# First tile's v loads moved to other queues, and w_in's first quarter issued between v's chunks

## The chip, the cores and the metric

The kernel runs on one core of one Trainium2 chip. The metric is the time of one execution on the device in microseconds (us). It is about 1.7 us longer than the span from the first to the last instruction, which is what the profile shows. Each ratio compares a kernel with runs of the kernel before on the same chip; the two chips are called A and B.

In the lines from profiles, PE is TensorE (the matmuls and transposes), ACT is ScalarE, DVE is VectorE, POOL is GpSimd and SP is SyncE; a q after the name (ACTq, SPq) is that engine's sequencer, here busy with issuing a transfer. PSUM is where this kernel keeps the tiles that PE writes (`hp`, `ops` and `sc` in the lines). The semaphore of a transfer is the number under which the trace records its landing; each load of the head has 16 updates there, and counts here as landed at the last. The granted clock is the profile's column of that name: 1.0 or 0.5 in these records. Fillers are matmuls whose result nobody uses.

## The reference, cut to what matters

```python
# q, k, v: 8 batches x 8 heads x 576 positions x 64, float32
scores = (1/sqrt(64)) * q @ k^T
ret    = scores * where(i >= j, gamma[h] ** (i - j), 0)     # retention: a decay per head
attn   = ret @ v
x      = attn as (4608 tokens, 512)
h      = x @ w_in                    # 512 x 2048
g      = h * tanh(softplus(h))       # Mish
out    = g @ w_out                   # 2048 x 512
```

## The kernel before

The tokens go in tiles of four chunks of 128 positions. The first tile's four chunks are the head of the kernel: nothing can be multiplied before their q and k are loaded, so that tile is loaded and prepared by its own code. q and k of a chunk are four transfers on SyncE's queue, and v is one on ScalarE's:

```python
def load_first(n):
    b, i0, _ = chunks[n][0]
    m, u = divmod(n, 2)
    for x, src in (("q", q), ("k", k)):
        heads = src.rearrange("b (p e) s d -> b e p s d", e=2)
        for e in range(2):
            nc.sync.dma_start(out=pairs[m][x][:, u, ds(4 * e, 4), :]..., in_=heads[b, e, :, ds(i0, P), :]...)
    nc.scalar.dma_start(out=pairs[m]["v"][:, u], in_=v[b, :, ds(i0, P), :].rearrange("h p d -> p h d"))

load_first(0)
# ...
keep_warm(12)                                     # filler matmuls on PE, so that it never stands idle for long
# ... small constants; two exponentials on ScalarE ...
nc.scalar.activation(gv, ex, AX.Exp, scale=-1.0)
nc.scalar.activation(gq, ex, AX.Exp)
nc.vector.tensor_scalar(gq, gq, 1.0 / math.sqrt(D), None, op0=OP.mult)
load_first(1)                                     # <- v1's issue stands here in ScalarE's queue
first = consts.tile([P, 1], F32)
nc.scalar.activation(first, pos[:, 0:1], AX.Mish) # fetches the Mish table early
```

A chunk then passes through these steps: P (VectorE scales q into bfloat16), C (GpSimd casts k), V (GpSimd scales v), T (transposes), S (scores and the mask), O (outputs). PE transposes q into a PSUM tile, ScalarE copies it out, and only then does PE write k's half of the same tile (in the profile of before the copy ends at 11.01 and k's transposes start at 11.05):

```python
tp = ps_h.tile([P, 2, NP, P], BF16, name="hp")
for i in range(2):                                # 0: q, 1: k
    for t in range(4):
        nc.tensor.transpose(tp[:, i, t, :], lines[:, ts(t, P)], ident)
    nc.scalar.copy(r["qk"][:, i, u]..., tp[:, i]...)
```

```python
one(0, "PCVT")
for n in range(NCH):                              # NCH = 4
    last = n == NCH - 1
    if n + 2 < NCH:
        load_first(n + 2)
    keep_warm(4)
    if not last:
        one(n + 1, "P")
    one(n, "S")
    keep_warm(3)
    if not last:
        one(n + 1, "C")
        if n == 2: load_w_in(2, 2)                # GpSimd's queue
        one(n + 1, "V")
        if n == 1: load_w_in(0, 2)
        one(n + 1, "T")
        one(n, "O")
```

After that loop come the w_in matmuls, the rest of the weights and the other tiles. The change leaves those as they were.

## Time and profile before

| of the kernel before | value |
|---|---|
| time, median of the first 3 runs | 324.58 us (323.99 to 324.62) |
| span of the profiled execution | 322.4 us, granted clock 0.995 |
| PE busy | 96% |
| PE idle between the transposes of q and of k of chunk 0 | 4.06 us |
| first w_in matmul | 25.51 us |

The prediction shows PE's side of the head. The other half is on ScalarE. This is its timeline before (columns: start in us, length, engine, line, operation, output<-input, count, and in brackets the idle time before it with what ended it):

```profile
4.16 0.22 ACT L193 ACTIVATE gq<-ex 128x40 f32<-128x40 f32 x1
8.62 0.38 ACTq L140 DMA_DIRECT2D vraw<-in_v_dram  x1
9.03 1.28 ACT L197 ACT_TABLE_LOAD   x1 [4.65 <-DMA qraw<-in_q_dram]
10.43 0.57 ACT L271 COPY qkT<-hp 128x512 bf16<-128x512 bf16 x1
```

ACTq is ScalarE's sequencer issuing a transfer. The idle time is put down beside the table load, yet what waited is the issue ahead of it. It asks for v and was released by a q transfer, which landed at 8.60, 0.02 us before it.

The page's table of DMA queues (packets, MB, share of the 16 engines' span) shows GpSimd's queue first and ScalarE's second; the last line below is the first w_in matmul in PE's timeline, the marker that I use for the end of the head:

```profile
q0 software_dynamic: 43104, 25.17, 53.7%
q10 hardware_dynamic: 25104, 6.42, 11.6%
...
25.51 1.46 PE L374 MATMUL hp<-xT,w_in_t 128*128 128x384 bf16 x8
```

### The profile page before, as it was taken

What the parts mean: (1) busy time and instruction counts of PE and PEld (TensorE: products, weight loads), DVE (VectorE), ACT (ScalarE), POOL (GpSimd) and SP (SyncE); (2) the same over time, 40 slices, a digit from 0 to 9 for tenths busy, and PEclk for the clock granted to TensorE, in tenths of its full rate; (3) what the DMA queues carried; (4) which work ended last, traced back from release to release, by engine and by line L of the source; (5) the groups of instructions that cost most, each with busy time, mean ns of one, the idle gap of its engine ahead of it and who ended that gap; (6) DMA issues with size and microseconds to landing.
All of it is one profiled execution on the core that took longest, in us unless ns stands there. A gap on an engine that the chain in (4) does not pass through costs nothing.

```text
span 322.4 us, 6091 instructions
## 1 busy us (share of the span) xinstructions
PE 308.9 (96%) x2648; PEld 160.9 (50%) x2648; DVE 131.0 (41%) x173; ACT 126.3 (39%) x208; POOL 79.9 (25%) x102
## 2 busy tenths in 40 slices
PE   7589999999999999899999999999999999999996
PEld 2245568945555554344545454445454544444444
DVE  5241274126664775172626263544444432000111
ACT  2445766603455541343434342434343432333200
POOL 4486783426430021404040404050000000000000
PEclk9799999999999999999999999999999999999999
DMA  6689999999999049496969969696040400001023
GB/s 177 181 125 212 216 200 220 200 202 250 212 238 158 35 98 181 101 194 150 222 95 201 134 146 167 144 147 150 33 100 33 100 33 35 33 34 35 33 70 93
DMA packets 75786, 43.38 MB, mean 135 GB/s; under 512 B 59760, under 2 KB 67184, under 8 KB 75760
## 3 DMA queue, kind: packets, MB, share of 16 engines
q0 software_dynamic: 43104, 25.17, 53.7%
q10 hardware_dynamic: 25104, 6.42, 11.6%
q1 hardware_dynamic: 7552, 11.41, 11.3%
q8 instruction: 20, 0.33, 0.5%
q14 instruction: 6, 0.05, 0.0%
HBM read 36.70 MB, written 9.44 MB: 143 GB/s over the span
## 4 chain that ended last, share of the span: by engine, by line
PE 90%; ACT 3%; ACTq 2%; SPq 2%; DVE 1%; DMA 1%; issue 0%
PE hp L363 33%; PE ops L401 31%; PE hp L401 5%; PE hp L386 4%; PE sc L299 3%; PE sc L348 3%; PE ops L152 2%; PE sc L341 2%; PE st L320 2%; ACTq L261 2%; PE sc L278 2%; SPq L138 2%; PE hp L413 1%; ACT qkT L279 1%; PE hp L374 1%; DMA qraw<-in_q_dram 1%
## 5 line engine op out<-in xcount | busy, mean ns | idle before, releaser
L363 PE MATMUL hp<-xT,w_in_t 128*128 128x512 bf16 x496 | 126.4, 380 | 1.7 <-ACT gT L365 1.7
L365 ACT ACTIVATE gT<-hp 128x512 bf16<-128x512 f32 x124 | 74.0, 598 | 130.8 <-PE hp L363 120.5
L401 PE MATMUL ops<-w_out_t,gT 128*128 128x512 bf16 x480 | 121.9, 379 | 0.0
L401 PEld LDWEIGHTS <-gT 128*128 128x128 bf16 x560 | 54.2, 98 | 64.7 <-issue 0.8
L421 DVE COPY res<-ops 128x512 f32<-128x512 f32 x30 | 20.7, 691 | 130.8 <-PE ops L401 130.8
L363 PEld LDWEIGHTS <-w_in_t 128*128 128x128 bf16 x496 | 46.0, 98 | 54.8 <-issue 2.2
L302 DVE TENSOR_TENSOR sm<-sc,mask 128x1024 bf16<-128x1024 f32 x36 | 42.7, 1217 | 27.6 <-PE sc L299 27.6
L533 POOL COPY seen<-qkT 1x1 bf16<-1x1 bf16 x10 | 1.8, 177 | 127.7 <-DMA qkT<-qks 127.7
L324 ACT ACTIVATE ssb<-st,diag 128x512 bf16<-128x512 f32 x32 | 20.2, 684 | 12.8 <-PE st L320 12.8
L352 DVE CAST xT<-sc 128x512 bf16<-128x512 f32 x32 | 20.8, 685 | 6.7 <-PE sc L348 5.9
L107 POOL DMA_DIRECT2D qraw<-in_q_dram x16 | 17.2, 1076 | 24.5 <-DVE qks L235 19.0
L252 DVE TENSOR_TENSOR vs<-vraw,gv 128x1024 bf16<-128x1024 f32 (+1 forms) x18 | 19.8, 1099 | 0.0
L235 DVE TENSOR_TENSOR qks<-qraw,gq 128x1024 bf16<-128x1024 f32 (+1 forms) x18 | 19.7, 1095 | 0.0
L401 PE MATMUL hp<-w_out_t,gT 128*128 128x512 bf16 x80 | 18.8, 380 | 0.0
L107 POOL DMA_DIRECT2D qks<-in_k_dram x16 | 17.3, 1083 | 5.3 <-DMA qraw<-in_q_dram 3.6
L107 POOL DMA_DIRECT2D vraw<-in_v_dram x16 | 17.4, 1095 | 3.0 <-DMA w_out_t<-in_moe_w_out_dram 2.0
L386 PE MATMUL hp<-xT,w_in_t 128*128 128x128 bf16 x272 | 16.9, 219 | 0.0
L279 ACT COPY qkT<-sc 128x1024 bf16<-128x1024 bf16 x12 | 12.1, 1014 | 11.7 <-PE sc L278 11.7
L386 PEld LDWEIGHTS <-w_in_t 128*128 128x128 bf16 x272 | 15.4, 98 | 0.8 <-issue 0.2
L152 PE MATMUL ops<-idle 128*128 128x512 bf16 x40 | 13.6, 482 | 1.3 <-DVE line L171 1.3
L348 PE MATMUL sc<-sm,vs 128*64 128x128 bf16 x288 | 13.8, 220 | 0.0
L299 PEld LDWEIGHTS <-qkT 64*128 64x128 bf16 x288 | 8.2, 95 | 10.1 <-issue 5.9
(67 smaller groups left out, 152.9 us busy)
## 6 DMA issues: line engine op xcount, KB each, us to landing
out_dram<-res SPq DMA_DIRECT2D x31, 256.0 KB, 3.4
qraw<-in_q_dram POOLq DMA_DIRECT2D x12, 512.0 KB, 6.4
vraw<-in_v_dram POOLq DMA_DIRECT2D x12, 512.0 KB, 9.4
qks<-in_k_dram POOLq DMA_DIRECT2D x12, 256.0 KB, 7.7
qraw<-in_q_dram POOLq DMA_DIRECT2D x8, 256.0 KB, 9.0
vraw<-in_v_dram POOLq DMA_DIRECT2D x8, 256.0 KB, 8.7
w_out_t<-in_moe_w_out_dram POOLq DMA_DIRECT2D x4, 512.0 KB, 11.2
qraw<-in_q_dram SPq DMA_DIRECT2D x8, 128.0 KB, 3.3
```

Of the source, the lines that this page charges most:

```text
L107: nc.gpsimd.dma_start(out=t[ds(off, ni)].rearrange("p u h d -> p (u h) d"), in_=src[ds(b, 2), :, ds(i0, ni), :].rearrange("b h p d -> p (b ...
L152: nc.tensor.matmul(warm, lhsT=idle[:, 0:P], rhs=idle, start=True, stop=True)
L252: (nc.gpsimd if early else nc.vector).tensor_tensor(r["vs"][:, u], r["v"][:, u], g, op=OP.mult)
L302: nc.vector.tensor_tensor(sm.rearrange("p e n i -> p (e n) i"), sc.rearrange("p e n i -> p (e n) i"), (mask if len(chunks[n]) == 1 else ma ...
L324: nc.scalar.activation(ssb[:, :, :, e, :], st, AX.Copy, scale=diag[:, e:e + 1])
L348: nc.tensor.matmul(ot[ds(64 * e, 64), p, :], lhsT=vs[:, u, 2 * p + e, :], rhs=sm[:, e, p, :], start=(start and p == 0), stop=True, skip_gr ...
L352: (nc.scalar.copy if t == 0 else nc.vector.tensor_copy)(xts[t][:, :, ts(s, P)], ot)
L363: nc.tensor.matmul(hp, lhsT=w_in_t[:, c, ts(f, P)], rhs=xts[t][:, c, :], start=(c == 0), stop=(c == KC - 1))
L365: nc.scalar.activation(gts[t][:, f, :], hp, AX.Mish)
L386: nc.tensor.matmul(hp[:, j, :], lhsT=w_in_t[:, c, ts(4 * fb + j, P)], rhs=xts[t][:, c, ts(s, P)], start=(c == 0), stop=(c == KC - 1))
L401: nc.tensor.matmul(ops, lhsT=gts[t][:, f, ts(s, P)], rhs=w_out_t[:, f, :], start=(f == 0), stop=(f == nF - 1))
L421: copy(ot, ops)
```

## The change

The intent is to take v's transfers out of the way of q, k and ScalarE. Two chunks of v are issued by ScalarE as its very first instructions, two by GpSimd once it has built its masks. SyncE then issues all of q and k in one go. The first two w_in transfers move a step earlier, behind each chunk's v scaling.

```diff
-        nc.scalar.dma_start(out=pairs[m]["v"][:, u], in_=v[b, :, ds(i0, P), :]...)
-    load_first(0)
+    def load_v(n, queue):
+        (b, i0, _), = chunks[n]
+        queue.dma_start(out=pairs[n // 2]["v"][:, n % 2], in_=v[b, :, ds(i0, P), :]...)
+    load_v(0, nc.scalar)
+    load_v(1, nc.scalar)
+    for n in range(NCH):
+        load_first(n)
 ...
-    keep_warm(12)
+    keep_warm(13)
 ...
-    load_first(1)
     first = consts.tile([P, 1], F32)
 ...
     nc.gpsimd.memset(mask2[0:64, 64:P], 0.0)
+    load_v(2, nc.gpsimd)
+    load_v(3, nc.gpsimd)
 ...
-        if n + 2 < NCH:
-            load_first(n + 2)
 ...
-            one(n + 1, "C")
-            if n == 2:
-                load_w_in(2, 2)
-            one(n + 1, "V")
-            if n == 1:
-                load_w_in(0, 2)
+            one(n + 1, "CV")
+            if n < 2:
+                load_w_in(2 * n, 2)
```

More of the change, by code (lines that the diff above doesn't have):

```diff
@@ L139, in load_first @@
                                   in_=heads[b, e, :, ds(i0, P), :].rearrange("p (g t) d -> g p (t d)", t=4))
-        nc.scalar.dma_start(out=pairs[m]["v"][:, u], in_=v[b, :, ds(i0, P), :].rearrange("h p d -> p h d"))
-    load_first(0)
+    def load_v(n, queue):
+        (b, i0, _), = chunks[n]
+        queue.dma_start(out=pairs[n // 2]["v"][:, n % 2], in_=v[b, :, ds(i0, P), :].rearrange("h p d -> p h d"))
+    load_v(0, nc.scalar)
+    load_v(1, nc.scalar)
+    for n in range(NCH):
+        load_first(n)
     idle = consts.tile([P, d_model], BF16)
```

## The prediction

> **What bounds the kernel now.** I read the page first. PE is busy 96% of the span and the chain that ended last is 90% PE; the only non-PE pieces are small. So a change of loads can win only where PE stands still, and part 2 of the page shows that in the first slices alone (8 us each, the first column is 0 to 8 us, the second 8 to 16):
>
> ```profile
> PE   7589999999999999899999999999999999999996
> PEclk9799999999999999999999999999999999999999
> DMA  6689999999999049496969969696040400001023
> PE 90%; ACT 3%; ACTq 2%; SPq 2%; DVE 1%; DMA 1%; issue 0%
> ```
>
> The second step is the chain of waits in order of time over the first 60 us (columns: start us, length us, what):
>
> ```profile
> 6.06 2.54 DMA qraw<-in_q_dram
> 8.60 0.02 issue
> 8.62 0.38 ACTq L140
> 9.00 0.03 issue
> 9.03 1.28 ACT L197
> 10.31 0.01 issue
> 10.32 0.20 ACT first L197
> 10.53 0.48 ACT qkT L271
> 11.01 0.04 issue
> 11.05 0.58 PE hp L269 x4
> 11.64 1.71 PE ops L152 x4
> ```
>
> Until 11 us the chain is not arithmetic. ScalarE has finished its small exponentials at 4.38; the next instruction on its queue is the issue of the second chunk's v (L140), which stands still until 8.60, when a q transfer that SyncE issued at 6.06 has landed. v1 does not need that q: in the compiled streams each DMA takes one of eight semaphores in turn and waits for its last user, and v1's number was last used by the third chunk's q. Behind it stand the Mish table load (1.28) and the first copy of q's transposes out of PSUM (10.43), which both need nothing but ScalarE. Third, the PE timeline shows what that costs:
>
> ```profile
> 1.26 5.30 PE L152 MATMUL ops<-idle 128*128 128x512 bf16 x12 [1.26 <-DVE line L171]
> 6.36 0.63 PE L269 MATMUL hp<-ident,qks 128*128 128x128 bf16 x4
> 11.05 0.58 PE L269 MATMUL hp<-ident,qks 128*128 128x128 bf16 x4 [4.06 <-ACT qkT L271]
> 11.43 1.91 PE L152 MATMUL ops<-idle 128*128 128x512 bf16 x4
> 16.20 1.04 PE L152 MATMUL ops<-idle 128*128 128x512 bf16 x4
> ```
>
> q's transposes are done at 6.99; k's go to the same PSUM tile and start at 11.05: 4.06 us idle. The four filler matmuls after it take 1.91 against 1.04 later: the clock fell. Narrow windows give a granted clock of 0.50 from 10.5 to 13.5 us.
>
> From then on the four first chunks follow PE, ScalarE and VectorE: transposes of q at 14.47, 18.15, 21.83 and the first w_in matmul at 25.51, a period of 3.67. After 26 us the waits of PE sum to 3.0 us, of which 1.7 is one stall at 128.9 behind a DMA transpose issued by ScalarE that took 6.32, and none waits for a load.
>
> [...] idle 6.99 to 11.05, clock 0.50 from about 10.4 to 13.7. [...] v0 (256 KB in 1024 packets of 256 B) moves from about 1.9 to 3.2 us and q0, issued at the same 0.81, starts only at about 3.0; while v1 moves (9.5 to 11.4) SyncE's queue falls from some 105 packets per half microsecond to 20 to 40. [...]
>
> **The change, part by part.**
>
> 1. ScalarE's queue. v0 and v1 are issued first of all (0.81 and about 1.25, 0.4 each) with no predecessor on their semaphores; v2 and v3 leave ScalarE. So ScalarE loses the wait of 4.24 (4.38 to 8.62) and two issues of 0.38. The table load runs at about 4.4 to 5.7, hidden, and the copy waits for the transposes alone. The first table load moves from 1.27 to 1.7 and ends at about 3.0, where gq waited for VectorE until 2.99 anyway: free.
>
> 2. q and k on SyncE. v1 now moves ahead of them or between them: 1.2 to 1.3 us later (v0's move took 1.9 to 3.2). q0 was landed at 5.05 (VectorE's first scaling started at 5.07 after a wait of 0.26), so now about 6.1 to 6.3; scaled (0.69) by 6.8 to 7.0. The thirteenth filler moves the end of the fillers by one spacing of 0.43 (5.1 for twelve starts) from 6.36 to 6.8. So q's transposes start at about 6.9 in place of 6.36.
>
> 3. v2 and v3 on GpSimd: two issues of about 0.9 (the rows of GpSimd's q, k and v issues say 0.88 to 0.92) at 3.1 to 5.0, before k0 is there (5.8 before). They add 512 KB to DMA engines whose share was 0.7 to 0.9 from 3.5 to 9 us, so k0 (landed at 5.8) may slip by 1.3 for v1 and some tenths for these: about 7.3, cast (0.61) by 7.9. Copy of q: transposes end about 7.35, copy 0.57 to about 7.9. k's transposes start at about 8.0 to 8.3 in place of 11.05. I take 8.2: gain 2.85.
>
> 4. The clock. [...] The stretch from k's transposes to the next q's transposes was 11.05 to 14.47 = 3.42; at full clock it is the same work as 15.54 to 18.15 = 2.61 without the eight output matmuls (0.34): 2.27. Gain 1.15. (Check by pieces: fillers 1.71 against 0.97, transposes 0.58 against 0.38, scores 0.54 against 0.33.)
>
> 5. The three later chunks keep 3.67 each. q and k of chunk 1 land by about 9 to 10.5, needed at 10.5 to 11.5; those of chunks 2 and 3 have 2 us or more. The w_in matmuls start at 8.2 + 2.27 + 3 x 3.67 = 21.5 instead of 25.5.
>
> 6. w_in's first quarter. Its two issues now stand after v1's and v2's scaling (about 11.5 and 14), where DMA was idle (share 0.01 to 0.2 at 14.5 to 18). GpSimd's later issues, 20.74 before, fall to about 16.3 to 17, so the eighths needed at 29.70 - 4 have the same nine microseconds as before (20.74 to 29.70). This part alone wins nothing: PE never waited for w_in; it keeps the earlier PE from waiting.
>
> Sum: 2.85 + 1.15 = 4.0 us. The instructions after 26 us are the same on every engine, and shift as a whole. 324.58 - 4.0 = **320.6 us**, 1.2% less.
>
> **Rivals.** (a) Loads become the bound of the head. v1, v2 and v3 together put 768 KB in front of or beside q and k. If they slow SyncE's queue to half from 4 us, q0 lands at 6.6 and k0 at 8.0, k's transposes start at 8.7 and chunk 1's at 11 or later: gain 2 to 3.5, time 321.1 to 322.5. For it: the starving of SyncE by v's packets; against it: later chunks have slack, and GpSimd's transfers start slowly (2.5 us from issue to first packet for w_in). (b) The expected best: k0 isn't delayed by GpSimd, k's transposes at 7.9: gain 4.4, 320.2. More is not there, as the fillers hold q to 6.8. (c) w_in's matmuls or the loads after them become late because GpSimd waits for v2 or v3 before its w_in issues, and gives the gain back: 322 to 324.5. Against it: v2 and v3 are issued at about 3 and 4 and wanted after 12; DMA stands idle before 18 now. (d) The single stall of 1.7 at 129 changes with the phase of transfers: plus or minus 1.7. (e) The clock isn't granted in the head[...]: minus 1.15 of the gain.
>
> **Range and chances.** Most weight on (b) to the centre and (a): 319.4 to 322.3. A gain of 2% needs 6.5 us, more than the whole idle gap (4.06) and the slow clock (1.15) together. A loss of 2% would need new waits of 10 us in the head; nothing points there. Faster 0.03, same 0.95, slower 0.02.
>
> **What would show it.** ScalarE's Mish table load at 4.4 to 5.7; its first copy at about 7.3; PE's idle time before the second group of transposes under 1.3 instead of 4.06, q's first transposes at 6.8 to 7.2; the second filler group near 1.0 instead of 1.91 and no 0.50 clock; q's transposes 3.67 apart; first w_in matmul at 21.2 to 22.2 instead of 25.51 and the same distance from there to the end (296.9). It is wrong if PE's transposes wait for q or k (rival a), if PE waits for w_in after 21 us (c), or if the distance from the first w_in matmul to the end changes by over half a microsecond (d).

The marked cuts are what was said of the hardware from elsewhere, without a trace or run of this case. They take no term out of the sum, which stands as 2.85 + 1.15 = 4.0 us, and so 320.6. That the clock would stay full without the gap was the estimate; the 1.15 itself is worked out from stretches of the profile (3.42 - 2.27). The semaphores can be read in the trace of before: the head's 20 transfers on the queues of SyncE and ScalarE use eight numbers (SyncE's sixteen go through them twice, in one order), and each of the twelve that use a number again is issued only after its last user has landed. For v1 that is 8.62 after 8.60.

## The result, and the profile after

The changed kernel took **320.25 us** (median of 4 runs, 320.08 to 321.84) against 324.60 (4 runs) of the kernel before. The ratio is 0.9876, with an interval of 0.9845 to 0.9906, so the class is "same" (within 2%). A ratio in this document is the mean time of one kernel's fast runs over that of the other's fast runs of the same rounds, so it is not quite the ratio of the medians quoted beside it. The outputs were correct, here and in every experiment.

The profiled run was the slowest of the changed kernel's five runs: 321.84 us where the others took 320.06 to 320.34. Its profile therefore shows a little more than the typical run has. I come back to this below.

The page after, the same parts as the prediction shows of before (busy tenths of PE, granted clock and DMA share over 40 slices of 8 us; then the chain by engine):

```profile
PE   6689999999999997999999999999999999999995
PEclk9999999999999999999999999999999999999999
DMA  8889999999997069597995959495040400000022
...
PE 90%; ACT 2%; DMA 2%; ACTq 2%; DVE 1%; SPq 1%; issue 0%; DVEq 0%
```

The clock's dip in the second slice is gone, and DMA is busier in the first two slices (8 and 8 tenths in place of 6 and 6). PE's first slice is not fuller than before (6 in place of 7): the thirteen fillers ended at 5.71, where the twelve of before ended at 6.56, and PE then stood idle for 1.06. The fillers start 0.43 us apart until 4.27 in this profile and 0.22 apart from then on; 4.27 is also where the trace's first record of the granted clock begins (6.98 in the profile of before). The chain has more DMA than it had (2% in place of 1%). So something was taken away and something else came.

What was taken away shows in ScalarE's timeline after:

```profile
4.36 0.22 ACT L199 ACTIVATE gq<-ex 128x40 f32<-128x40 f32 x1
4.60 1.28 ACT L202 ACT_TABLE_LOAD   x1
5.89 0.20 ACT L202 ACTIVATE first<-pos 128x1 f32<-128x1 f32 x1
7.21 0.58 ACT L278 COPY qkT<-hp 128x512 bf16<-128x512 bf16 x1 [1.11 <-PE hp L276]
```

The table load follows the exponentials at once, and the copy now waits for PE's transposes, as it should. What came shows in PE's timeline:

```profile
6.77 0.40 PE L276 MATMUL hp<-ident,qks 128*128 128x128 bf16 x4 [1.06 <-DVE qks L238]
7.84 0.38 PE L276 MATMUL hp<-ident,qks 128*128 128x128 bf16 x4 [0.67 <-ACT qkT L278]
8.06 1.03 PE L158 MATMUL ops<-idle 128*128 128x512 bf16 x4
...
11.54 0.40 PE L276 MATMUL hp<-ident,qks 128*128 128x128 bf16 x4 [1.37 <-DVE qks L238]
...
22.58 1.46 PE L381 MATMUL hp<-xT,w_in_t 128*128 128x384 bf16 x8
```

k's transposes start at 7.84 instead of 11.05, and the four fillers after them take 1.03 instead of 1.91. But the next chunk's transposes of q start only at 11.54, after 1.37 us of idle time. VectorE's timeline says why, and the chain of waits names the transfer (start, length, what):

```profile
10.79 0.69 DVE L238 TENSOR_TENSOR qks<-qraw,gq 128x512 bf16<-128x512 f32 x1 [4.08 <-DMA qraw<-in_q_dram]
...
4.12 6.57 DMA qraw<-in_q_dram
```

A half of chunk 1's q, issued at 4.12, landed 6.57 us later. The packet records say what moved beside it. From 5.7 to 9.2 us, while GpSimd's v2 and v3 move, SyncE's queue starts 413 packets of 1024 bytes beside 126 of GpSimd's with 4096, which is 59 of its own per half microsecond; from 9.2 to 11.7, beside 2 of GpSimd's, it starts 778, or 156 per half microsecond. In the profile of before, where v2 and v3 do not move from 5.7 to 9.2 us, SyncE's queue starts 705 there, or 101 per half microsecond. So it starts fewer while v2 and v3, the only new traffic of that time, move. But that is not what made this one half so late. The trace has 16 updates of its semaphore. Fifteen had come by 8.63, and the last came at 10.70. The halves after it also lack their last update for some 0.9 us (the next: 11.08, after 10.14). Two of GpSimd's packets, started one after the other at 5.89 and 7.02, took 1.14 and 0.79 us where the median is 0.20. In the second profile of the same kernel (below), with the same v2 and v3, no such packet took over 0.34 and this half had landed whole by 8.58. So one part of the sixteen lagged in this run, and the record does not show why. The queue table shows v2 and v3 change place:

```profile
q0 software_dynamic: 43264, 25.69, 54.4%
...
q10 hardware_dynamic: 23024, 5.90, 11.3%
```

ScalarE's queue lost 0.52 MB, and GpSimd's gained it. By the packet records 2048 packets of 256 bytes became 128 of 4096; the rest of the difference in the counts is packets of 4 bytes.

The head ended 25.51 - 22.58 = 2.93 us earlier. The span fell by only 2.3 (322.4 to 320.1), because the one stall of PE later on, behind a DMA transpose of ScalarE, was 2.2 in place of 1.7.

### The profile page after: what moved, and what is told of

The parts are those of the page before. It is cut to its first block, busy times and chain, and to the rows that moved or that the text cites. A ratio compares the mean times of both kernels' runs of the same rounds, so it can differ in the third digit from the quotient of the medians.

```text
span 320.1 us, 6094 instructions
## 1 busy us (share of the span) xinstructions
PE 306.9 (96%) x2649; PEld 160.1 (50%) x2649; DVE 131.9 (41%) x173; ACT 126.2 (39%) x208; POOL 82.1 (26%) x104
## 3 DMA queue, kind: packets, MB, share of 16 engines
q1 hardware_dynamic: 7552, 11.41, 11.5%
## 4 chain that ended last, share of the span: by engine, by line
PE 90%; ACT 2%; DMA 2%; ACTq 2%; DVE 1%; SPq 1%; issue 0%; DVEq 0%
PE hp L370 33%; PE ops L408 31%; PE hp L408 6%; PE hp L393 4%; PE sc L306 3%; PE sc L355 3%; DMA qraw<-in_q_dram 2%; PE sc L348 2%; ACTq L268 2%; PE st L327 2%; PE ops L158 2%; PE sc L285 2%; PE hp L420 1%; SPq L138 1%; ACT qkT L286 1%; PE hp L381 1%
## 5 line engine op out<-in xcount | busy, mean ns | idle before, releaser
L286 ACT COPY qkT<-sc 128x1024 bf16<-128x1024 bf16 x12 | 12.1, 1014 | 11.7 <-PE sc L285 11.7
L158 PE MATMUL ops<-idle 128*128 128x512 bf16 x41 | 11.9, 424 | 1.3 <-DVE line L177 1.3
```

## The experiments

There were twelve runs of kernels, the first four on chip A, the rest on chip B. The kernel before had a median of 324.43 on A and 324.62 to 324.70 on B, which varies with the rounds. The theory was: ScalarE stands behind v1's issue, and that false wait, with the clock lost in the idle time it makes, is the whole gain; v2 and v3 on GpSimd and w_in's new place add nothing. The main rivals were that the gain comes from v arriving sooner, or from GpSimd's share of the work, or from the clock alone.

### The changed kernel once more

> The changed kernel once more, to see whether the profiled run of 321.84 us (its four other runs were 320.06 to 320.34) is typical. In it chunk 1's q landed at 10.7 us, 6.6 after its issue, and PE stood 1.37 us before chunk 1's q transposes (11.54). Theory A: that late landing is an accident of contention with the two v loads of GpSimd, and a run of 320.1 to 320.3 has it at 9 to 9.6 us, q transposes of chunk 1 at 10.1 to 10.2 and the first w_in matmul at 21.1 to 21.3. Rival B: the head is as in the first profile (22.58) and the 1.7 us lie elsewhere, at the stall of 2.2 us behind ScalarE's DMA transpose near 126 us.

No edit. It took 319.94 (ratio 0.9849, 0.982 to 0.9877). This profiled run was typical (319.48), and its PE timeline after k's transposes at 7.77 reads:

```profile
9.93 0.39 PE L276 MATMUL hp<-ident,qks 128*128 128x128 bf16 x4
11.27 0.40 PE L276 MATMUL hp<-ident,qks 128*128 128x128 bf16 x4 [0.95 <-POOL qks L248]
...
21.26 1.46 PE L381 MATMUL hp<-xT,w_in_t 128*128 128x384 bf16 x8
```

Here q of chunk 1 was in time, and only its k, cast by GpSimd, was late: PE waited 0.95, where 0.67 is the usual wait for ScalarE's copy, so 0.28 was lost. The late q of the first profile is thus not in every run. (The forecast had q's transposes at 10.1 to 10.2.) The first w_in matmul came 4.25 us earlier than before, and the sum closes: 11.05 - 7.77 = 3.28 for the start, plus 3.42 - 2.16 = 1.26 for the faster stretch to chunk 1's transposes (7.77 to 9.93), minus 0.28.

### v by ScalarE alone: two early, two late

```diff
-    load_v(2, nc.gpsimd)
-    load_v(3, nc.gpsimd)
 ...
 for n in range(NCH):
+    if n + 2 < NCH:
+        load_v(n + 2, nc.scalar)
     keep_warm(4)
```

> The changed kernel, but v2 and v3 stay on ScalarE's queue at their old places; only v1's early issue is kept. Theory A (the false wait of ScalarE is the whole cause): 320.0 to 320.6, ratio to the kernel before 0.987, first w_in matmul at 21.1 to 21.6, and no late q of chunk 1. Rival: GpSimd's taking of two loads carries part of the gain; then 321.5 or more.

It took 319.50 (0.9846, 0.9809 to 0.9882), against 319.94 of the changed kernel on the same chip. That is a little below the forecast of 320.0 to 320.6. So v1's early issue carries all of the gain, and GpSimd's share is not needed. SyncE issues q and k at the same times here as in the kernel before (0.81, 2.19, 3.48, 4.77, 6.06, 7.36, within 0.01), so having them "in one go" changed nothing either. Its first w_in matmul is the earliest of the three:

```profile
21.03 1.46 PE L379 MATMUL hp<-xT,w_in_t 128*128 128x384 bf16 x8
```

That is 4.48 before the old 25.51: 11.05 - 7.83 = 3.22 for k's transposes, and 1.25 for the stretch after (7.83 to 10.00). v2's issue came at 8.82, 0.02 us after the q transfer that had last used its semaphore had landed (8.80). So this issue was held too, for about 0.5 us, as v1's was before; it cost nothing, since ScalarE's next copy waits for PE until 10.42. And k of chunk 1 landed whole at 8.46; with v2 and v3 by GpSimd it was 10.48 in the second profile of the changed kernel. That is what GpSimd's share costs.

> The kernel of the earlier run in which v2 and v3 stay on ScalarE's queue (319.50 there), again, beside the next two on one chip: 319.2 to 319.9, first w_in matmul at 20.9 to 21.3.

The same kernel on chip B, in five rounds, took 319.46 (0.9837, 0.9814 to 0.9859). It reproduces.

### v2 and v3 by GpSimd alone, on top of the kernel before

```diff
+        if n < 2:
+            load_v(n, nc.scalar)          # v0 and v1 where they were
 ...
     nc.gpsimd.memset(mask2[0:64, 64:P], 0.0)
+    load_v(2, nc.gpsimd)
+    load_v(3, nc.gpsimd)
```

> The kernel before, with only v2 and v3 moved to GpSimd; v1 stays behind its wait on ScalarE. Theory A: ScalarE's wait remains to about 8.6 us or later (the third chunk's q is slowed by two more loads), so 324.3 to 325.5, no gain. Rival (relieving ScalarE's queue of two issues and loading v early carries the gain): 322 or less.

It took 327.48 (1.0093, 1.0052 to 1.0134), so it is about 3 us worse than the kernel before, and 2 worse than the upper end of the forecast (324.3 to 325.5). Some of that is the clock, whose mean was 0.977 to 0.990. ScalarE's timeline and then PE's:

```profile
10.89 0.43 ACTq L145 DMA_DIRECT2D vraw<-in_v_dram  x1
11.35 1.28 ACT L202 ACT_TABLE_LOAD   x1 [6.82 <-DMA qraw<-in_q_dram]
...
13.37 0.59 PE L276 MATMUL hp<-ident,qks 128*128 128x128 bf16 x4 [6.93 <-ACT qkT L278]
```

The q transfer that v1's issue waits for is now slower: 4.8 us from issue to landing, the longest of q's transfers in this run, where it took 2.54 before. The early v2 and v3 are the only change. The issue moves from 8.62 to 10.89 and PE's gap grows from 4.06 to 6.93. The parts of the change do not add up: this one loses 3 us alone, and 0.4 to 0.7 once v1 no longer waits.

### The gap kept, PE kept busy in it

```diff
     for t in range(4):
         nc.tensor.transpose(tp[:, i, t, :], lines[:, ts(t, P)], ident)
+    if n == 0 and i == 0:
+        keep_warm(14)                     # the second version: 19
```

> The kernel before with 14 filler matmuls between the q and the k transposes of chunk 0, so that PE is busy through ScalarE's wait and the clock stays granted; nothing else changes. If the clock is worth the predicted 1.15 us: 323.2 to 323.7, first w_in matmul at 24.3 to 24.6, the second filler group at 1.04 in place of 1.91. If the clock costs nothing beyond the gap: 324.3 to 324.9.

> The kernel before with 19 fillers in the gap in place of the 14 of the earlier run, whose fillers ended at 9.1 us and whose profiled run (324.38) lost the clock at 11 us although its three other runs (322.2 to 322.8) had a mean clock of 0.998 to 1.0. With PE busy to 10.2 or later the clock stays: all runs at 322.0 to 322.8, mean clock 0.998 or more, first w_in matmul at 24.2 to 24.5, second filler group at 1.04. If the gain of 1.9 came from anything else than the clock, the profile shows where.

These leave v1's issue where it was and test the clock alone. Fourteen fillers were too few. In the profiled run PE still stood idle for 2.30 us after them, and the next fillers took 1.91: the clock was lost all the same (0.58 in the mean from 11 to 14 us), and that run took 324.38. The three other runs took 322.17 to 322.80 with clocks of 0.998 to 1.0. The median was 322.49 (0.994, 0.99 to 0.9981), below the forecast of 323.2 to 323.7. Nineteen settle it: 322.09 (0.9919, 0.9894 to 0.9944), with the granted clock at 0.999 to 1.0 in every run. In the profiled one they kept PE busy to 10.41:

```profile
11.17 0.38 PE L269 MATMUL hp<-ident,qks 128*128 128x128 bf16 x4 [0.76 <-ACT qkT L273]
11.39 1.03 PE L152 MATMUL ops<-idle 128*128 128x512 bf16 x4
...
13.34 0.39 PE L269 MATMUL hp<-ident,qks 128*128 128x128 bf16 x4
```

k's transposes come as late as ever (11.17), yet the stretch from them to the next q is 2.17 instead of 3.42. Here the clock alone is worth 1.25 us.

By the medians it is 324.70 - 322.09 = 2.6, and most of the difference can be found. The trace's records of the granted clock have the low clock in pieces: 3.41 us in the profile of before (10.40 to 13.81), none with nineteen fillers. By an estimate from that length, one such piece at half clock makes a mean of 1 - 0.5 x 3.41 / 322.4 = 0.995, two make 0.989, three 0.984. The 23 runs of before beside the experiments (11 on A, 12 on B) lie in just these groups:

| mean clock | pieces of 3.41 us | runs of before | median us |
|---|---|---|---|
| 0.993 to 0.995 | one | 6 | 324.16 |
| 0.988 to 0.989 | two | 14 | 324.60 |
| 0.983 | three | 3 | 326.54 |

So the profiled run of before (0.995, 324.13) was one of the better ones. The profiled pair differs by 324.13 - 322.58 = 1.55; the typical run of before adds 0.5 for a second piece; and the profiled run with nineteen fillers was 0.5 slower than its own median. That makes the 2.6. That each group has that number of pieces is worked out from the means; only the first is in a profile. The mean also leaves out the time before the first record of the clock (6.98 in that profile), when the fillers are 0.43 us apart.

### The Mish table ahead of v1's issue

```diff
-    load_first(1)
     first = consts.tile([P, 1], F32)
     nc.scalar.activation(first, pos[:, 0:1], AX.Mish)
+    load_first(1)
```

> The kernel before, with the Mish table load put ahead of v1's issue on ScalarE, so that 1.28 us of table load and 0.2 of activation run during the wait; the two copies still stand behind the issue. Theory A (ScalarE's queue in order, standing behind v1's wait): the copy of q starts at 9.0 to 9.1 in place of 10.43, k's transposes at 9.6 to 9.7, gain 1.4, and as the gap shrinks to 2.7 us the clock may stay granted, up to 1.15 to 2 more: 321.0 to 323.0. If the copy starts at once after the transposes (7.0), the wait isn't what holds ScalarE.

It took 323.84 (0.9959, 0.9921 to 0.9997) with runs of two kinds: 322.71 and 322.72 at a mean clock of 0.995, 325.78 and 324.96 at 0.983. ScalarE's timeline of the profiled one, which was the slowest:

```profile
4.39 1.28 ACT L196 ACT_TABLE_LOAD   x1
...
9.10 0.37 ACTq L140 DMA_DIRECT2D vraw<-in_v_dram  x1
9.51 0.58 ACT L271 COPY qkT<-hp 128x512 bf16<-128x512 bf16 x1 [3.62 <-DMA qraw<-in_q_dram]
```

The table load is out of the way, and the copy still stands behind the issue until 9.51. From the end of the issue to the copy it is 0.04 us instead of 1.43 (9.00 to 10.43), so the table was worth 1.4; k's transposes came only 0.9 earlier (10.15 for 11.05; forecast 9.6 to 9.7), because v1's issue itself came 0.48 later in this run. So the gap was 3.63 and not the forecast's 2.7, and the clock was lost. With one piece of low clock this kernel is at 322.7 against 324.16 of before, which agrees. The forecast of 321.0 to 323.0 holds for those two runs and not for the median. What remains is the issue, and it is the cause.

This run also lost the clock for longer, 10.24 us in one stretch from 9.31 to 19.55, which is three pieces. Its matmuls agree: the four fillers at 16.56 took 1.89 where 1.04 is usual.

Why three pieces here and one in the profile of before, after nearly the same gap (3.63 and 4.06)? No run shows it. What the traces give is PE's busy time in the 3.41 us ahead of the low clock and in the low pieces themselves (columns: ahead, in the low pieces, and in brackets the share of 3.41):

| profile | PE busy ahead | PE busy in the low pieces |
|---|---|---|
| before | 0.01 us (0%) | 2.76 (81%) |
| table first, this run | 0.62 (18%) | 2.57 (75%), 2.74 (80%), all of the third |
| fourteen fillers | 1.12 (33%) | all of the one piece, from about 11.5 to 14.9 |

In the changed kernel's first profile PE was busy for 1.84 us (54%) from 4.27 to 7.68, and the clock stayed at 1.0. These few pieces do not show how much busy time keeps the clock or brings it back, and the ends of matmuls in a trace are modelled. What they do show is that nearly the same gap cost one piece in one run and three in another.

### w_in's first quarter in its old place

```diff
-            one(n + 1, "CV")
-            if n < 2:
-                load_w_in(2 * n, 2)
+            one(n + 1, "C")
+            if n == 2: load_w_in(2, 2)
+            one(n + 1, "V")
+            if n == 1: load_w_in(0, 2)
```

> The changed kernel with w_in's two first issues at the places of the kernel before (w_in 0 and 1 after v2's scaling, w_in 2 and 3 between chunk 3's cast and scaling). Prediction's step 6 says that the place wins nothing by itself but keeps the earlier PE from waiting. If no wait: 319.8 to 320.4, same as the changed kernel. If the place matters: w_in 2 and 3 issued near 16, needed at 23.0, a PE wait for w_in of 0.3 us or more and 320.5 or more.

It took 320.20 on chip B (0.9859, 0.9834 to 0.9883), as forecast. PE never waits for w_in in its profile. The changed kernel took 320.25 and 319.94 in its own sets, so the new place is worth nothing that can be measured. On chip B this kernel, which is the changed one in all but w_in's place, is 0.7 above v by ScalarE alone (319.46); the runs of the two don't overlap (319.98 to 320.48, 319.21 to 319.82). Its k1 landed at 10.71 and PE lost 0.33 to it.

### All of v on SyncE, each behind its q and k

```diff
-    load_v(0, nc.scalar)
-    load_v(1, nc.scalar)
     for n in range(NCH):
         load_first(n)
+        load_v(n, nc.sync)
 ...
-    load_v(2, nc.gpsimd)
-    load_v(3, nc.gpsimd)
```

> The changed kernel with all four v on SyncE's queue, each behind its chunk's q and k: nothing on ScalarE's or GpSimd's queue, and v1 not early. Theory A (only ScalarE's wait mattered, not v early, not the queue that carries it): 319.0 to 320.0, q0 landing at 4 to 5 in place of 6, chunk 0's q transposes at 5.8 to 6.7 behind the fillers, first w_in matmul at 20.3 to 21.3. Rival: v must be early or spread over queues; then PE waits for vs or for k of a later chunk and the time is 321 or more.

It took 319.75 (0.9848, 0.9824 to 0.9871). Nothing of v is on ScalarE, and v1 is not early, and the gain is the same. So an early v is not the cause; an unblocked ScalarE is. Its profiled run was its slowest (321.0, clock 0.995, the others 319.06 to 320.04). It started q's transposes at 6.21, waited 1.80 for a late k of the last chunk, and lost one piece of clock after it (the four fillers at 19.87 took 1.89, the three at 22.23 1.02), so its first w_in matmul came at 23.09 where 20.3 to 21.3 was forecast. In that one run the delay by loads did appear; the other five have no profile.

### Versions meant to beat both

> An attempt at beating both: q0 and k0 issued first on two queues, the rest in order of need on SyncE, Mish table load behind chunk 0's copies, chunk n's v scaled after chunk n+1's k cast, 8 fillers and 2 between the q and k transposes, w_in spread earlier. If the head is bound by the landing of q0 and k0: q transposes at 4.7 to 5.0, k transposes at 5.8 to 6.2, first w_in matmul at 19.1 to 19.8, 317.5 to 318.5. If w_in or loads of later chunks become the bound: PE waits between 8 and 24 us, 318.5 to 321.

The first put chunk 0's k on ScalarE's queue beside q on SyncE's and each v two chunks late on SyncE's, and used eight fillers. It also moved the Mish table behind chunk 0's copies, put two fillers between the transposes, scaled v a chunk later and loaded w_in earlier, so the miss can't be put down to one of these. It took 320.61 (0.9868, 0.9846 to 0.9891): a miss. In its profile VectorE scaled q at 5.29, behind its own small instructions; the fillers had ended by then, PE stood idle for 1.77 and the clock fell: the four fillers at 7.68 took 1.91, those at 12.87 1.04. Later k3 came late for GpSimd, but all that PE lost there was 0.21 for a scaled v.

The second and third keep q and k first on SyncE with v0 and v1 behind them, and have GpSimd issue v2 and v3 only after its first v scaling and its second cast. They differ in the fillers, ten and twelve (cut: v3's issue after chunk 1's cast of k, the old issues of v that go, and w_in's 4 to 7 ahead of chunk 3's cast):

```diff
+    for n in range(NCH):
+        load_first(n)
+        if n < 2:
+            load_v(n, nc.sync)
 ...
+    one(0, "PCV"); load_v(2, nc.gpsimd); one(0, "T")
```

> Second attempt at beating both: v0 and v1 on SyncE's queue behind their q and k, so that q0 lands near 4.8 and not 6; v2 and v3 issued by GpSimd after chunk 0's scaling and chunk 1's cast; 10 fillers; w_in 4 to 7 issued before chunk 3's cast. If the landing of q0 and k0 sets the start: q transposes at 5.6 to 5.8, k transposes at 6.6 to 6.9, first w_in matmul at 19.9 to 20.3, 318.2 to 318.9. Rival: fewer fillers leave the clock ungranted, or k of a later chunk comes late behind GpSimd's transfers: PE waits for the k cast or a granted clock of 0.5 after 7 us, and 319.3 or more.

> The same with 12 fillers in place of 10. If the clock decides, better than the one with 10: 318.4 to 319.2, with q transposes at 5.7 to 6.4; if not, 0 to 0.6 us worse than it.

They took 319.38 (0.9835, 0.981 to 0.986) and 319.37 (0.983, 0.9806 to 0.9855), where 318.2 to 318.9 and 318.4 to 319.2 were forecast: both missed. Two fillers more or less made no difference. The second starts q's transposes at 5.46, 1.3 us before v by ScalarE alone, but most of that is given back. Its waits over the first 40 us (engine and line, what it waited for: us in total, times, longest) have

```profile
PE hp L274 <- POOL qks L246: 2.9, 3, 1.3
```

Each of the three waits would have been 0.67 for ScalarE's copy, so 0.9 is lost to GpSimd's casts of k, which PE waits for next. First w_in matmul: 20.68, against 21.03. In time neither version can be told from v by ScalarE alone (319.46). The changed kernel itself was not timed on chip B; with w_in in its old place, which costs nothing, it took 320.20 there, and all three are 0.7 to 0.8 below that. On chip A, v by ScalarE alone was 0.44 below the changed kernel by the medians, though there the single runs overlap.

## Why the prediction was right, point by point

The time lay 0.35 us below the predicted 320.6 and inside the range. The mechanism, v1's issue and the clock, was right and is shown; that the number came so close is partly luck, as the steps show. Three small readings in the prediction are a little off: while v1 moved before, SyncE's queue started 14 to 35 packets per half microsecond and not 20 to 40 (from 10.5 to 11.0 it was 14 of 1024 bytes beside 491 of ScalarE's with 256), the low clock ended at 13.81 and not about 13.7, and k0 had landed at 5.68 and not 5.8. None of them carries the sum.

- **Step 1, ScalarE's queue: right and shown.** The table load ran at 4.60 (predicted 4.4), the copy at 7.21 waited for PE alone. Early v1 alone gives the whole gain, all of v off ScalarE gives it too, and GpSimd's part alone makes v1's wait longer and loses 3 us.
- **Step 2, q's transposes at 6.9: right** (6.77 and 6.70 in the two profiles). The predicted cause held in the first profile, where PE waited for VectorE's scaling, which waited for q behind v. In the second the fillers held it. They ended at 5.71 in the first and at 6.65 in the second.
- **Step 3, k's transposes at 8.2: a little too late.** They came at 7.84 and 7.77, so this term was worth 3.2 to 3.3 rather than 2.85. k0 was delayed, but by less than predicted: it landed at 6.75 in the first profile (5.68 before, 7.3 predicted), and PE did not feel it, as it waited only the 0.67 of ScalarE's copy. As far as k's transposes go this was rival (b), the expected best.
- **Step 4, the clock: right in the profile, too small in typical runs.** The term was 1.15, and with the gap gone the clock stayed full (1.0 and 0.999 in the two profiled runs, the four fillers in 1.03). Nineteen fillers measured 1.25 in the profile and 2.6 by the medians. The predicted number was drawn from one profiled run, with one piece of low clock; 17 of the other 23 runs of before had two or three by their mean clocks.
- **Step 5, chunk 1 in time: the step that failed.** The prediction had q and k of chunk 1 land by 9 to 10.5 with something to spare. In the first profile q landed at 10.70, and the stretch to q's transposes was 11.54 - 7.84 = 3.70 instead of 2.27: 1.4 lost, to the last of the transfer's sixteen updates, as fifteen were there by 8.63. In the second profile k1 landed at 10.48, inside the predicted time, but the head had started earlier and it was now needed by about 10.3: 0.28 lost (0.33 with w_in in its old place). With v2 and v3 on ScalarE k1 landed at 8.46 (GpSimd's cast of it began at 8.58, and at 10.61 in the second profile) and nothing was lost. This is rival (a), moved from chunk 0 to chunk 1, and its sign, PE waiting for q or k, was there in both profiles. The first w_in matmul, at 22.58 and 21.26, was outside the predicted 21.2 to 22.2 once and inside once. The periods of 3.67 after it held (11.54, 15.23, 18.90, 22.58).
- **Step 6, w_in: right.** Its old place gives the same time, and PE waits for w_in in neither.
- **Rival (c)** did not come: no waits for w_in. **Rival (d)** came at its size: the distance from the first w_in matmul to the end of the span was 296.9 before, 297.5 and 296.3 after, and that stall 1.7, 2.2 and 1.2. By the prediction's own sign, a change over half a microsecond, it came in both profiles (0.6 more, 0.6 less). With the stall taken off, all three are within 0.2 of each other.

The sum was thus right partly because errors offset each other, which is luck: the start and the clock were worth more than predicted, the loads of v2 and v3 took something back. The two profiles of the changed kernel differ by 2.5 us (spans of 320.1 and 317.6): 1.3 of it lies in the head, where q was late, and 1.2 after it, of which the one stall is 1.0. The other runs of the first set have no profile. A lost piece of clock is not what made the first run 321.84: its clock was 1.0. (The one run of 321.54 of v by ScalarE alone was at 0.995, so that one did lose a piece.)

## What to carry to other kernels

When an engine's first compute instruction starts late, look at what stands ahead of it in its own queue: an issue of a transfer held it for 4.2 and 6.4 us here on behalf of a transfer it has nothing to do with, so such issues belong at the very start of the queue (319.50 here) or on an engine that computes nothing (319.75), where the kernel before took 324.43 and 324.62. Test the parts of a change alone: here one part carried all of the gain, one took 0.4 to 0.7 of it back, and one did nothing that could be measured. And measure the clock's share by filling the gap with work rather than closing it, since a single profile can understate it (1.25 here, and 2.6 by the medians).
